# A fused attention and mixture-of-experts kernel: the first q and k transfers issued by two engines

## The chip, the cores and the metric

The kernel runs on one core of a Trainium2 chip. A core has TensorE (PE, matrix products and transposes), VectorE (DVE), ScalarE (ACT), GpSimd (POOL), SyncE (SP, which issues transfers) and 16 DMA engines that all of the core's transfers share. The metric is the device time of one execution in microseconds (us); lower is better. Times of the profile count from the first instruction of the profiled execution.

## The reference

Sliding-window attention with a few "sink" keys, then two mixture-of-experts layers over its output:

```python
scores = scale * np.matmul(q, k.transpose(0, 1, 3, 2))          # (2, 8, 768, 64) q, k, v
keep = (pos[None, :] < n_sink) | ((rel >= 0) & (rel < window))  # n_sink = 4, window = 128
scores = np.where(keep, scores, -1e9)
a = softmax(scores)                                             # rows, 1e-9 added to the sum
x = a @ v                                                       # -> (1536, 512)
x = sum over 4 experts of p[:, e] * (relu(x @ w1[e]) @ w2[e])
x = for each token, its best of 8 experts: gate * (relu(x @ w1b[e]) @ w2b[e])
```

`n_sink` and `window` are inputs, two 64-bit integers in HBM: the kernel reads them on the chip, builds its masks from them, and chooses between a narrow path (taken here) and a general one.

## The kernel before

The program runs in three stages: attention over eight pairs of heads (to about 120 us), the first expert layer (about 120 to 680 us), the second one with its routing (to the end). The change lies in the first ten microseconds, in `Attention.__init__`, before the planned loop over the pairs of heads.

For the first pair (`g = 0`) q and k come in two halves of the sequence: `h0` is the first three blocks of 128 positions, `h1` the last three. `load(g, n, z)` issues two transfers, one for each head of the pair (`x` = 0, 1); `n` is 0 for q and 1 for k. A transfer of one half and one head is 128 x 3 x 64 floats, 98,304 bytes. `ksr` holds the first eight keys of all 16 heads (8 x 16 x 64 floats, 32,768 bytes); `words` gets `n_sink` and `window`, each broadcast to 128 partitions as 8 bytes.

All of these are issued on SP, in the order in which they are written. Each transfer signals its landing on one of eight semaphores (DMAHW0 to DMAHW7) that are used in turn. A transfer that takes a semaphore for the second time is not issued before the first transfer on it has landed: the issuing engine stands and waits.

PE starts with 26 products of a zero tile (`busy`, tile `dum`), whose result nobody reads. Then, written out by hand:

- PE transposes the first half of q (L324), runs 6 idle products, transposes the first half of k (L338) and the first pair's eight sink keys (L340, it needs `ksr`), and runs 18 idle products;
- ScalarE loads its function table for the exponential (L242, with a one-element activation `warm`), then rounds the transposed q (`q_hi`, L328) and the transposed k with its sink keys (`k_hi`, L343);
- VectorE forms the remainder of q (`q_lo`, L332), then turns `words` into floats (L140 to L143), computes the flag `fi` that chooses the path (L269 to L272), forms the remainder of k (`k_lo`, L347) and makes the masks (L291 to L294);
- every engine loads `fi` into a register (`values_load`, L276). On PE this load stands behind the 18 idle products and ahead of the transposes of the second half of q, so PE's further work waits for `fi`.

From there on an event planner (`Order`) has set the order; it is the same before and after.

Of the kernel before, what the change touches and what calls it, by code (L numbers as in the profile page):

```python
# [29 lines left out]
NS = 8  # L30
# [38 lines left out]
class Constants:  # L69


    def __init__(s, nc, cp, ident, emb, tau, probs, en):
        s.nc, s.cp, s.ident, s.en = nc, cp, ident, en
        s.p = cp.tile([P, NT, E1], F32, name="pr")
        s.ta = cp.tile([E2, 1], F32, name="ta")
        nc.sync.dma_start(out=s.p, in_=probs.rearrange("(t p) e -> p t e", p=P))
        s.emb = emb
        nc.sync.dma_start(out=s.ta, in_=tau.partition_broadcast(E2))

        def iota(name, shape, pattern, base, cm):  # L80
            t = cp.tile(shape, F32, name=name)
            nc.gpsimd.iota(t, pattern=pattern, base=base, channel_multiplier=cm, **IOTA)
            return t

        s.w8 = iota("w8", [P, 4, E2], [[0, 4], [-1, E2]], E2, 0)
        s.row = iota("row", [P, P], [[1, P]], 0, 0)
        s.col = iota("colc", [P, E2 * NT], [[1, E2 * NT]], -E2 * NT, 0)
        s.tok = iota("tok", [P, NT], [[P, NT]], 1, 1)
        s.slot = cp.tile([1, NT - 1], F32, name="slotn")
        nc.gpsimd.iota(s.slot, pattern=[[P, NT - 1]], base=P, channel_multiplier=0, **IOTA)  # L90
        s.one = cp.tile([P, 1], F32, name="one")
        nc.gpsimd.tensor_scalar(s.one, s.tok[:, 0:1], 1.0, None, ALU.is_equal)
        s.tr = iota("tr", [P, P], [[1, P]], 0, -1)
        s.tri = cp.tile([P, P], BF16, name="tri")
        s.on = cp.tile([P, P], BF16, name="on")
        s.enT = cp.tile([P, 4, E2], F32, name="enT")
        nc.gpsimd.tensor_scalar(s.tri, s.tr, 0.0, None, ALU.is_gt)
        nc.gpsimd.memset(s.on, 1.0)
# [37 lines left out]
def int64_as_float(nc, tp, i, n):  # L136

    V = nc.vector
    f = tp.tile([P, n, 2], F32, name="i64f")
    V.tensor_copy(f, i)  # L140
    t = tp.tile([P, n], F32, name="i64t")
    V.scalar_tensor_tensor(t, f[:, :, 0], 0.0, f[:, :, 1], ALU.is_lt, ALU.add)
    V.scalar_tensor_tensor(t, t, 4294967296.0, f[:, :, 0], ALU.mult, ALU.add)  # L143
    return t
# [62 lines left out]
class Attention:  # L207


    def __init__(s, tc, st, c0, ps, q, k, v, n_sink, window, x, ident):  # L210

        s.tc, s.nc = tc, tc.nc
        s.q, s.k, s.v, s.x, s.ident = q, k, v, x, ident
        nc = s.nc
        c1 = st.enter_context(tc.tile_pool(name="a1", bufs=1))
        s.qk = [[c1.tile([P, 6, 2, HD], F32, name=f"{n}r{i}") for i in range(2)] for n in "qk"]
        s.vt = [c1.tile([P, 6, 2, HD], F32, name=f"vt{n}") for n in range(3)]
        s.qs = [c1.tile([P, 2, S], F32R, name=f"qs{n}") for n in range(2)]
        s.kk = [c1.tile([P, 2, 2, KW // 2], F32R, name=f"kk{n}") for n in range(2)]
        s.ksr = c1.tile([NS, NH, HD], F32, name="ksr")  # L220
        s.vsr = [c1.tile([P, 4, P], F32, name=f"vsr{n}") for n in range(2)]
        s.pp = ps.tile([P, 2, 512], F32, name="prep")
        s.xo = [ps.tile([P, 512], F32, name=f"xo{a}") for a in range(2)]
        V, A, G = nc.vector, nc.scalar, nc.gpsimd
        s.dum = c1.tile([P, P], BF16, name="dum")
        V.memset(s.dum, 0.0)
        s.busy(s.xo[1], 26)
        words = c0.tile([P, 2, 2], I32, name="words")
        h0, h1 = slice(0, 3), slice(3, 6)
        s.load(0, 0, h0)  # L230
        s.load(0, 1, h0)
        for i, src in enumerate((n_sink, window)):
            nc.sync.dma_start(out=words[:, i], in_=src.bitcast(I32).partition_broadcast(P))
        nc.sync.dma_start(out=s.ksr, in_=k[:, :, 0:NS, :].rearrange("b h s d -> s (b h) d"))
        s.load(0, 0, h1)
        s.load(0, 1, h1)
        s.load(1, 0)
        s.load(1, 1)
        s.vload(0)
        e = c1.tile([1, 1], F32, name="warm")  # L240
        V.memset(e, 0.0)
        A.activation(e, e, AF.Exp)  # L242
        s.rel = c1.tile([P, 2 * P], F32, name="rel")
        s.key = c1.tile([P, P], F32, name="key")
        G.iota(s.rel, pattern=[[-1, 2 * P]], base=P, channel_multiplier=1, **IOTA)
        G.iota(s.key, pattern=[[1, P]], base=0, channel_multiplier=0, **IOTA)
        G.affine_select(
            out=s.rel, in_=s.rel, pattern=[[-1, 2 * P]], compare_op=ALU.is_ge, fill=3.0e38, base=P, channel_multiplier=1
        )
        s.sk = [c1.tile([P, 4, 32], F32, name=f"sk{n}") for n in range(2)]  # L250
        s.masks = c1.tile([P, 4, W], F32, name="masks")
        for t in s.sk:
            G.memset(t, 0.0)
        for t in s.vsr:
            G.memset(t, 0.0)
        G.memset(s.masks[:, 0, P:], -1.0e30)
        G.memset(s.masks[:, 1, 2 * P :], -1.0e30)
        s.q_pe(0, s.pp[:, 0], 0)
        s.busy(s.xo[1], 6)
        s.k_pe(0, s.xo[0], 0)  # L260
        s.busy(s.xo[1], 18)
        s.q_hi(0, s.pp[:, 0], 0)
        s.k_hi(0, s.xo[0], 0)
        s.q_lo(0, s.pp[:, 0], 0)
        nw = int64_as_float(nc, c0, words, 2)
        s.nsf, s.wf = nsf, wf = nw[:, 0:1], nw[:, 1:2]
        fl = c1.tile([1, 2], F32, name="fl")
        fi = c1.tile([1, 1], I32, name="fi")
        V.tensor_scalar(fl[:, 0:1], nsf[0:1], float(NS), None, ALU.is_le)  # L269
        V.tensor_scalar(fl[:, 1:2], wf[0:1], -1.0, 128.0, ALU.mult, ALU.add)  # L270
        V.scalar_tensor_tensor(fl[:, 1:2], wf[0:1], -1.0, fl[:, 1:2], ALU.add, ALU.mult)
        V.scalar_tensor_tensor(fi, fl[:, 1:2], 0.0, fl[:, 0:1], ALU.is_ge, ALU.mult)  # L272
        s.k_lo(0, s.xo[0], 0)
        s.make_masks(c1)
        s.vsload(0)
        s.narrow = nc.values_load(fi[0:1, 0:1], min_val=0, max_val=1)  # L276
# [22 lines left out]
        A.copy(masks[:, 3, P : P + NS], snk[:, :NS])  # L299
        A.copy(masks[:, 3, P + NS :], win[:, P:])  # L300

    def load(s, g, n, z=slice(0, 6)):
        b, h0 = divmod(g * 2, H)
        for x in range(2):
            s.nc.sync.dma_start(
                out=s.qk[n][g % 2][:, z, x, :], in_=(s.q, s.k)[n][b, h0 + x].rearrange("(c p) d -> p c d", p=P)[:, z]
            )

# [840 lines left out]
class Moe2:  # L1149
# [113 lines left out]
    def second(s, w, x, fl, more):  # L1263
# [16 lines left out]
        s.slot(x, w, hooks)  # L1280

    def begin(s, psT, w, x, own, load):

        V, A, G, R = s.nc.vector, s.nc.scalar, s.nc.gpsimd, s.R
# [259 lines left out]
```

## Time and profile before

| | |
|---|---|
| median of 3 runs | 895.85 us (894.11 to 896.01) |
| profiled execution | 898.2 us, of which its span from first to last instruction 896.4 us |
| PE | busy 869.3 us, 97% of the span |
| VectorE, ScalarE, GpSimd | 417.4, 302.1 and 193.1 us |
| mean granted clock of PE | 0.987 of full speed |

In the timeline a row is a start, a duration, an engine, the line of the kernel, the operation, what it writes and reads, and in brackets how long the engine was idle before it and what ended that. "SPq" rows are transfers being issued, not the transfers themselves. In the table of windows each row is a stretch of time: its length, then the busy time of each engine, then the granted clock of PE (1.00 is 2.4 GHz, 0.50 is 1.2 GHz), the busy share of the DMA engines and GB/s.

### The profile page before, as it was taken

Reading aid. Unit: us, or ns where it says so; the run is one execution under the profiler, and the core shown is the slowest. Engines: PE = TensorE matmul, PEld = TensorE weight load, DVE = VectorE, ACT = ScalarE, POOL = GpSimd, SP = SyncE. Lnnn points to the kernel's source line nnn. Section 1 sums busy time; section 2 is a strip of 40 time slices with the busy share of each in tenths; the row PEclk is TensorE's granted clock in tenths of the full one; section 3 lists DMA queues with packets and bytes.
Section 4 is the critical chain, followed back from the end, with each engine's and each line's share of the span. In section 5 each row is a group of like instructions: output and inputs, shape, how many; then the busy total and the mean of one; then the engine's idle time right before and its main releaser. Section 6 shows DMA issues by size and latency. Waiting matters only on the chain. (4 is left out here: it accounts for less than half of the span.)

```text
span 896.4 us, 11797 instructions
## 1 busy us (share of the span) xinstructions
PE 869.3 (97%) x4266; PEld 681.0 (76%) x4266; DVE 417.4 (47%) x1003; ACT 302.1 (34%) x662; POOL 193.1 (22%) x291
## 2 busy tenths in 40 slices
PE   8999999999999999999999999999999799999995
PEld 6676777878888888888888888888887577777774
DVE  5787753121233121233121234858646768937510
ACT  5787852010302010302010303111233557636421
POOL 4576510000000000000000000030223846726310
PEclk8999999999999999999999999999999999999998
DMA  7567110030022000023000022101345577946200
GB/s 135 107 137 154 46 46 2 1 119 1 0 94 94 1 0 1 1 94 94 1 1 1 0 71 84 58 0 48 118 136 170 163 254 222 307 141 205 70 32 24
DMA packets 84400, 72.47 MB, mean 81 GB/s; under 512 B 43860, under 2 KB 68436, under 8 KB 84328
## 3 DMA queue, kind: packets, MB, share of 16 engines
q1 hardware_dynamic: 81448, 65.25, 25.0%
q0 software_dynamic: 2880, 6.30, 2.1%
q8 instruction: 40, 0.66, 0.3%
q14 instruction: 32, 0.26, 0.1%
HBM read 67.58 MB, written 7.09 MB: 83 GB/s over the span
## 5 line engine op out<-in xcount | busy, mean ns | idle before, releaser
L998 PE MATMUL ph<-x,wA 128*128 128x512 f32 x1152 | 273.0, 397 | 1.5 <-DVE h L1004 1.5
L1082 PE MATMUL po<-wA,h 128*128 128x512 f32 x1152 | 273.3, 396 | 0.0
L998 PEld LDWEIGHTS ph<-x,wA 128*128 128x128 f32 x1152 | 216.5, 188 | 54.2 <-DVE h L1004 1.9
L1082 PEld LDWEIGHTS po<-wA,h 128*128 128x128 f32 x1152 | 215.1, 188 | 51.7
L1003 ACT ACTIVATE h<-ph 128x512 fp32r<-128x512 f32 x96 | 57.4, 598 | 389.4 <-PE ph L998 384.1
L1004 DVE SCALAR_TENSOR_TENSOR h<-ph,h 128x512 fp32r<-128x512 f32 x96 | 66.4, 692 | 175.9 <-ACT h L1003 175.9
L60 POOL TENSOR_TENSOR gn<-gn,rss 128x4 f32<-128x4 f32 x9 | 1.8, 198 | 444.1 <-DVE gn L58 443.6
L682 DVE TENSOR_TENSOR wA<-raw,wA 128x512 fp32r<-128x512 f32 x107 | 77.3, 750 | 2.5 <-ACT wA L676 1.7
L1092 DVE SCALAR_TENSOR_TENSOR acc<-po,pr,acc 128x512 f32<-128x512 f32 x36 | 27.0, 750 | 109.9 <-PE po L1082 109.9
L676 ACT CAST wA<-raw 128x512 fp32r<-128x512 f32 x115 | 65.5, 618 | 4.0 <-DMA raw<-in_moe_w_dram 3.6
L408 POOL TENSOR_TENSOR P<-P,r 128x264 f32<-128x264 f32 (+1 forms) x87 | 54.2, 647 | 43.9 <-DVE r L403 24.5
L1219 PE MATMUL po<-wA,ht 128*128 128x512 f32 x216 | 58.3, 409 | 0.6 <-DVE ht L1213 0.6
L1213 DVE TENSOR_TENSOR ht<-hT,ht 128x512 fp32r<-128x512 f32 x30 | 20.7, 691 | 67.9 <-ACT ht L1212 67.8
L389 ACT ACTIVATE P<-m,nm 128x264 f32<-128x264 f32 x96 | 49.0, 512 | 8.3 <-DVE nm L383 7.8
L1219 PEld LDWEIGHTS po<-wA,ht 128*128 128x128 f32 x216 | 39.7, 192 | 9.4 <-DVE ht L1213 1.5
L383 DVE CUSTOM_DVE_ANT_0 m<-sc,masks 128x264 f32<-128x264 f32 x96 | 38.5, 429 | 14.0 <-PE sc L370 12.3
L1196 PE MATMUL ph<-wA,xt 128*128 128x512 f32 x168 | 42.7, 401 | 2.0 <-PEq L1346 1.0
L682 DVE TENSOR_TENSOR wB<-raw,wB 128x512 fp32r<-128x512 f32 x44 | 40.3, 940 | 4.4 <-ACT wB L676 3.3
L771 DVE CUSTOM_DVE_ANT_0 rj<-acc,raw 128x512 f32<-128x512 f32 x64 | 40.1, 687 | 0.2
L370 PE MATMUL sc<-kk,qs 64*128 64x264 f32 x288 | 38.2, 329 | 0.7 <-DVE nm L383 0.7
L1219 PE MATMUL po<-wB,ht 128*128 128x512 f32 x144 | 38.6, 405 | 0.3 <-DVE ht L1213 0.3
L1196 PEld LDWEIGHTS ph<-wA,xt 128*128 128x128 f32 x168 | 30.6, 188 | 10.7 <-DVE xt L1122 1.9
(220 smaller groups left out, 852.1 us busy)
## 6 DMA issues: line engine op xcount, KB each, us to landing
raw<-in_moe_w_dram SPq DMA_DIRECT2D x96, 512.0 KB
vt<-in_v_dram SPq DMA_DIRECT2D x16, 192.0 KB
xs<-acc SPq DMA_DIRECT2D x12, 256.0 KB
qr<-in_q_dram SPq DMA_DIRECT2D x14, 192.0 KB
kr<-in_k_dram SPq DMA_DIRECT2D x14, 192.0 KB
raw<-en SPq DMA_DIRECT2D x4, 512.0 KB
vsr<-in_v_dram SPq DMA_DIRECT2D x64, 2.0 KB
qr<-in_q_dram SPq DMA_DIRECT2D x4, 96.0 KB
```

The costliest lines, as they stand in the source:

```text
L383: V.tensor_tensor_reduce(m, t["sc", par][:, :W], masks[:, VAR[i]], -1.0, 3.0e38, ALU.add, ALU.min, t["nm"][:, par, i : i + 1])
L389: A.activation(t["P"][:, par, i], t["m", par, i], AF.Exp, scale=-1.0, bias=t["nm"][:, par, i : i + 1], accum_out=t["su"][:, par, i : i + 1],)
L408: eng.tensor_tensor(y, y, t["r", a][:, par].unsqueeze(2).to_broadcast([P, b - a, W]), ALU.mult)
L676: eng.copy(dst()[:, 0], r)
L682: eng.tensor_tensor(d[:, 1], r, d[:, 0], ALU.subtract)
L771: s.nc.vector.tensor_tensor_reduce(j, s.acc[:, tt], s.eb[e], 1.0, 0.0, ALU.mult, ALU.add, s.dl[:, tt, e : e + 1])
L998: s.nc.tensor.matmul(ph, s.wA.w1(a, k, f * P)[:, :P], s.x[:, b, k, tb * TB : (tb + 1) * TB], start=(n == 0), stop=(n == 11))
L1003: s.nc.scalar.activation(t[:, 0], ph, AF.Relu)
L1004: s.nc.vector.scalar_tensor_tensor(t[:, 1], ph, 0.0, t[:, 0], ALU.max, ALU.subtract)
L1082: nc.tensor.matmul(po, hs[f][:, a, t * P : (t + 1) * P], wA.w2(b, f), start=(n == 0), stop=(n == 23))
L1196: nc.tensor.matmul(ph[b], x[:, a, kk], w.w1(c, kk, b * 512), start=(kk == 0 and n == 0), stop=(kk == 3 and n == 2),)
L1219: nc.tensor.matmul(s.po[0], ht[b][:, a, c * P : (c + 1) * P], w.w2(d, f), start=(f == 0 and n == 0), stop=(f == 7 and n == 2),)
```

## The change

ScalarE issues the transfers of the second head of the first pair (`x = 1`), for both halves of q and k; SP keeps those of the first head. `ksr` moves to ScalarE, behind the first halves and ahead of the second halves. The two scalar inputs, which were issued between the halves, now come behind the second halves, still on SP. Nothing is added or taken away: there are as many transfers as before, with the same bytes.

```diff
         h0, h1 = slice(0, 3), slice(3, 6)
-        s.load(0, 0, h0)
-        s.load(0, 1, h0)
+        two = (nc.sync, nc.scalar)
+        s.load(0, 0, h0, two)
+        s.load(0, 1, h0, two)
+        nc.scalar.dma_start(out=s.ksr, in_=k[:, :, 0:NS, :].rearrange("b h s d -> s (b h) d"))
+        s.load(0, 0, h1, two)
+        s.load(0, 1, h1, two)
         for i, src in enumerate((n_sink, window)):
             nc.sync.dma_start(out=words[:, i], in_=src.bitcast(I32).partition_broadcast(P))
-        nc.sync.dma_start(out=s.ksr, in_=k[:, :, 0:NS, :].rearrange("b h s d -> s (b h) d"))
-        s.load(0, 0, h1)
-        s.load(0, 1, h1)
         s.load(1, 0)
         s.load(1, 1)
-    def load(s, g, n, z=slice(0, 6)):
+    def load(s, g, n, z=slice(0, 6), queues=None):
         b, h0 = divmod(g * 2, H)
         for x in range(2):
-            s.nc.sync.dma_start(
+            (queues or [s.nc.sync] * 2)[x].dma_start(
```

ScalarE at the start of the program, before (in these listings a row is a line of the kernel, an operation, what it writes and reads and its shape; the semaphores that it waits for stand in brackets; `qr` and `kr` are q and k as they come in):

```order
L242 ACT_TABLE_LOAD
L242 ACTIVATE warm<-warm 1x1 [waits DVE_49]
L328 ACTIVATE qs_97<-prep 128x384 [waits PE_49]
L343 CAST kk_99<-xo_105 128x392 [waits PE_49]
L295 COPY masks<-win 128x128 [waits DVE_49]
```

and after:

```order
L306 DMA qr_90<-in_q_dram 128x3x64
L306 DMA kr_92<-in_k_dram 128x3x64
L233 DMA ksr<-in_k_dram 8x16x64
L306 DMA qr_90<-in_q_dram 128x3x64 [waits DMAHW2_49]
L306 DMA kr_92<-in_k_dram 128x3x64 [waits DMAHW4_49]
L243 ACT_TABLE_LOAD
L243 ACTIVATE warm<-warm 1x1 [waits DVE_49]
L329 ACTIVATE qs_97<-prep 128x384 [waits PE_49]
L344 CAST kk_99<-xo_105 128x392 [waits PE_49]
```

Five transfers now stand ahead of the table load and of `q_hi`, and the last two of them wait for earlier transfers to land.

SP at the start of the program, before:

```order
L305 DMA qr_90<-in_q_dram 128x3x64 x2
L305 DMA kr_92<-in_k_dram 128x3x64 x2
L233 DMA words<-in_n_sink_dram 128x2
L233 DMA words<-in_window_dram 128x2
L234 DMA ksr<-in_k_dram 8x16x64
L305 DMA qr_90<-in_q_dram 128x3x64
L305 DMA qr_90<-in_q_dram 128x3x64 [waits DMAHW0_49]
```

and after:

```order
L306 DMA qr_90<-in_q_dram 128x3x64
L306 DMA kr_92<-in_k_dram 128x3x64
L306 DMA qr_90<-in_q_dram 128x3x64
L306 DMA kr_92<-in_k_dram 128x3x64
L237 DMA words<-in_n_sink_dram 128x2
L237 DMA words<-in_window_dram 128x2 [waits DMAHW0_49]
L306 DMA qr_91<-in_q_dram 128x6x64 [waits DMAHW1_49]
```

The two scalar inputs still stand behind four transfers of 98,304 bytes on SP; the second one has got a wait for the first transfer of q.

PE after, at the transposes of the first half of k, where the semaphores of k and of `ksr` can be read:

```order
L339 MATMUL xo_105<-ident,kr_92 128x128 [waits DMAHW3_49,DMAHW2_49]
L339 MATMUL xo_105<-ident,kr_92 128x128 x2
L341 MATMUL xo_105<-ident,ksr 128x8 [waits DMAHW4_49]
L285 LDWEIGHTS dum
L285 MATMUL xo_106<-dum 128x128
```

PE's own order has not moved; DMAHW2 and DMAHW3 belong to the first half of k, DMAHW4 to `ksr`.

## Rows read from the trace of the kernel before

**Rows 1.** The page, sections 1 and 2: PE's share, granted clock in 40 slices.

```profile
PE 869.3 (97%) x4266; PEld 681.0 (76%) x4266; DVE 417.4 (47%) x1003; ACT 302.1 (34%) x662; POOL 193.1 (22%) x291
PEclk8999999999999999999999999999999999999998
```

**Rows 2.** Table of windows over the attention stage; its first line names the columns.

```profile
core 0: us, PE busy (x) PEld busy (x) DVE busy (x) ACT busy (x) POOL busy (x), PEclk, DMA share, GB/s
0.00:10.00 10.00, 6.78 (x60) 6.06 (x60) 2.90 (x14) 2.82 (x6) 3.69 (x19) 0.94 0.62 119
10.00:20.00 10.00, 9.07 (x54) 6.51 (x52) 7.69 (x34) 7.54 (x25) 5.48 (x13) 0.84 0.80 128
...
30.00:60.00 30.00, 30.00 (x251) 20.91 (x250) 23.63 (x95) 24.20 (x72) 19.18 (x35) 1.00 0.47 106
```

**Rows 3.** Timeline of the first microseconds: transfers as SP issues them.

```profile
0.83 0.97 SPq L305 DMA_DIRECT2D qr<-in_q_dram  x2
...
1.84 1.02 SPq L305 DMA_DIRECT2D kr<-in_k_dram  x2
...
2.90 0.49 SPq L233 DMA_DIRECT2D words<-in_n_sink_dram  x1
...
3.43 0.43 SPq L233 DMA_DIRECT2D words<-in_window_dram  x1
...
3.91 0.38 SPq L234 DMA_DIRECT2D ksr<-in_k_dram  x1
```

**Rows 4.** The same timeline: PE's products and transposes.

```profile
1.07 2.96 PE L284 MATMUL xo<-dum 128*128 128x128 bf16 x26 [1.07 <-DVE warm L241]
...
4.17 0.87 PE L324 MATMUL prep<-ident,qr 128*128 128x128 f32 x3
...
5.45 0.50 PE L338 MATMUL xo<-ident,kr 128*128 128x128 f32 x3
...
7.95 0.22 PE L340 MATMUL xo<-ident,ksr 8*128 8x8 f32 x1 [2.01 <-DMA ksr<-in_k_dram]
...
8.11 1.48 PE L284 MATMUL xo<-dum 128*128 128x128 bf16 x18
...
9.38 0.85 PE L324 MATMUL prep<-ident,qr 128*128 128x128 f32 x3
```

**Rows 5.** The same timeline: ScalarE and VectorE.

```profile
0.81 1.28 ACT L242 ACT_TABLE_LOAD   x1 [0.81 <-PEq L1539]
...
2.10 0.20 ACT L242 ACTIVATE warm<-warm 1x1 f32<-1x1 f32 x1
...
5.08 0.49 ACT L328 ACTIVATE qs<-prep 128x384 fp32r<-128x384 f32 x1 [2.77 <-PE prep L324]
...
5.60 0.56 DVE L332 SCALAR_TENSOR_TENSOR qs<-prep,qs 128x384 fp32r<-128x384 f32 x1 [4.58 <-ACT qs L328]
...
7.45 0.17 DVE L140 CAST i64f<-words 128x4 f32<-128x4 int32 x1 [1.29 <-DMA words<-in_window_dram]
...
8.46 0.15 DVE L272 SCALAR_TENSOR_TENSOR fi<-fl 1x1 int32<-1x1 f32 x1
```

**Rows 6.** Instructions on tile fi, durations ns min/median/max, then starts: PE's register load.

```profile
L276 PEldq TENSOR_LOAD <-fi x1: 497/497/497, 8.7 to 8.7; - x1
```

**Rows 7.** Table of windows, columns as in rows 2: what the transfers moved.

```profile
1.90:2.90 1.00, 1.00 (x12) 1.00 (x11) 0.00 (x0) 0.39 (x2) 1.00 (x4) 1.00 0.68 155
2.90:3.90 1.00, 1.00 (x11) 0.86 (x9) 0.00 (x0) 0.00 (x0) 0.78 (x4) 1.00 0.80 181
...
4.40:6.40 2.00, 1.55 (x12) 1.25 (x11) 0.56 (x1) 0.49 (x1) 0.00 (x0) 1.00 0.05 1
...
9.40:11.40 2.00, 2.00 (x13) 1.43 (x12) 1.00 (x5) 1.58 (x7) 1.91 (x9) 0.50 1.39 219
```

**Rows 8.** Timeline: six score products at the low and at the full clock.

```profile
10.16 1.03 PE L370 MATMUL sc<-kk,qs 64*128 64x264 f32 x6
...
14.80 0.64 PE L370 MATMUL sc<-kk,qs 64*128 64x264 f32 x6
```

## The prediction

> **What bounds the kernel now.** I read the page first: PE is busy for 97% of the span and its clock is full except near the start and the end [rows 1]. The table of windows then says where a change of the first transfers can still matter: from 30 to 60 us PE is busy for 30.00 of 30.00 us, while in the first ten it lacks 3.2 us and in the next ten 0.9 [rows 2]. So PE is the bound of the whole attention stage, its order is fixed, and a microsecond won or lost before PE's first real work is carried on to the end, nearly one to one. The question is only when PE gets going.
>
> The timeline of the first ten microseconds answers that, and the reader is to look for the wait that ends last, not for the longest one. The longest is plain: PE has transposed the first half of k at 5.95 and stands still for 2.01 us until `ksr` lands at 7.95 [rows 4]. But behind it stand 18 idle products, to 9.59, and behind those the load of `fi`, which PE performs from 8.7 to 9.2; only then come the transposes of the second half of q, at 9.38 [rows 4, 6]. `fi` is written at 8.46 to 8.61 by VectorE, at the end of a chain that began at 7.45, when `words` had landed [rows 5]. Thus two transfers gate PE here: `ksr` at 7.95, and `words` at 7.45, whose chain of 1.16 us and register load end at about the same time as the idle products behind `ksr`. Take away one, and the other still holds PE until about 9.3.
>
> **What the change does to `ksr`.** It is issued as ScalarE's third transfer, at about 1.8 instead of 3.91 (two issues of about 0.5 us ahead of it, by SP's pace of 0.97 for two [rows 3]). It no longer stands behind `words`. That matters: from 4.40 to 6.40 the DMA engines moved 1 GB/s at a share of 0.05, though more transfers had been issued, so the two small broadcasts passed alone and held up what stood behind them on SP [rows 3, 7]. From issue to use the first q pair took 4.14 - 1.3 = 2.8 us for its second transfer, `ksr` itself 7.95 - 3.91 = 4.0 us [rows 3, 4]. Landing of `ksr` after: between 1.8 + 2.8 = 4.6 and 1.8 + 4.0 = 5.8. I take 4.9, near the lower end, because no broadcast stands ahead of it. Either end is before 5.95, where PE wants it: the wait of 2.01 us is gone, the 18 idle products run from about 6.15 to 7.6, and `k_hi` is done early. The gain on PE's path is nothing, since PE then stands at the load of `fi`.
>
> **What it does to q and k.** Two issuers at 0.5 us each bring the pairs out in half the time. It hides behind the 26 idle products, which run to 4.03 while the transposes of q start at 4.17 [rows 4]: at most 0.1 us, and not on the path.
>
> **What it does to `words`.** They are issued at the same place on SP, behind four transfers of 98,304 bytes, so at 2.90 and 3.43 as before. The second now waits for the first q transfer to land; by 0.83 + 2.8 = 3.6 that adds 0 to 0.2 us. What is new is the company: before, 393,216 bytes were ahead of them and had passed by 4.4, at 155 and 181 GB/s, the pace of one issuer [rows 7]. After, ScalarE's first two transfers and `ksr` pass at the same time, 622,592 bytes in all. At the 219 GB/s that the engines gave when they had enough to do [rows 7] this takes 2.8 us from 1.9, to 4.7. So `words` move later by 0.3, with bounds of 0 (the other queue doesn't disturb them) and 0.9 (ScalarE's second halves get between them too: 196,608 bytes more at 219 GB/s).
>
> Here a page bears on the case. The Trainium skill, "DMA: Bandwidth & Descriptors", section "Issuing engines are not separate DMA queues", says that transfers of all issuers run on the same 16 DMA engines and interleave, and that a second issuer saves only issue time. By that rule `words` go to the 0.3 and 0.9 ends; without it they stay at 0.
>
> **What it does to ScalarE.** This is the added wait. Five transfers stand ahead of the table load, and behind it `q_hi`. The fourth waits for a first-half transfer of k, the fifth for `ksr`. Behind them queue the table load, `warm`, `q_hi` and `k_hi` on ScalarE; behind `q_hi` VectorE's `q_lo`, and in VectorE's order the cast of `words` comes after `q_lo`. The chain, from rows: k lands at about 1.3 + 2.8 = 4.1, the fourth issue takes until 4.6; `ksr` at 4.9, the fifth issue until about 5.45; table load 1.28, to 6.73; `warm` 0.20, to 6.95; `q_hi` 0.49, to 7.45; `q_lo` 0.56, to 8.0 [rows 5]. Before, `q_lo` ended at 6.16, long before `words`. The cast therefore starts at 8.0 instead of 7.45: +0.55. With `ksr` at 4.6 it is +0.25, with 5.8 it is +1.45. The table load alone used to cost nothing, because ScalarE had nothing else to do from 0.81 to 5.08; that cover is gone.
>
> A second page would make this longer. The Trainium skill, "ScalarE: Activation LUTs", section "What ACT_TABLE_LOAD costs", gives 1283 ns for the load, as here, and a drain of about 1380 ns besides. In this trace the next activation began at 2.10, right behind the load [rows 5], so no drain shows; by the page the cast would start 1.38 us later still.
>
> **The sum.** The cast starts at the later of `words` (7.45 + 0.3) and `q_lo` (+0.55): +0.55. From there VectorE's chain to `fi`, PE's register load and the second half of q follow as before. `k_lo` gains 0.1 (its input is ready before `fi`), but the first scores wait for PE's transposes, so that gives nothing. PE's idle gap moves from 5.95..7.95 to about 7.6..9.8 and stays about as long. The granted clock fell to 1.2 GHz after the old gap: windows of 9.4 to 11.4 show 0.50 [rows 7], and six score products took 1.03 us there against 0.64 at the full clock [rows 8]. With a gap as long, I take the same fall, a little later, and no change from it. Everything later on SP (second pair, v) is issued earlier and is not waited for. The profiled execution: 898.2 + 0.55 = 898.75. The median of the runs shown is 2.35 below the profiled execution; with the same step it becomes 895.85 + 0.55 = 896.4.
>
> **The rivals.** What a measurement of this kernel can tell from no change is about 0.2%, 1.8 us, so the bounds are 894.05 and 897.65.
>
> - *ScalarE becomes the gate for good* (slower). Its place is the fifth transfer, which waits for `ksr`. If `ksr` lands late, the table load, `q_hi`, `q_lo`, the cast and `fi` all move with it, one to one. It decides from the point where the cast starts at 7.45 + 1.8 = 9.25, that is with `ksr` at about 6.2. If `ksr` lands as late as before, at 7.9, the chain reads 8.45, 9.73, 9.95, 10.45, 11.0: +3.55, 899.4. For it: the engines are shared, and the only landing of `ksr` in this trace took 4.0 us. Against it: these 4.0 us contain the 2.0 us of the broadcasts, which stand behind it now. At 4.0 us from its new issue it still lands at 5.8. Chance 0.15.
> - *The table load drains* (slower): q_lo ends at 8.0 + 1.38 = 9.4 and the sum is +1.95, 897.8, just beyond the bound. The row on `warm` speaks against it. Chance 0.03.
> - *The clock doesn't fall* (faster). PE is busy from 1.07 to 7.6 without the 2.01 us gap, and the later gap could end before the clock falls. Then three groups at the start of the second ten (transposes of q and of k, six scores) each gain about 0.35 to 0.4, 1.1 us, and the low stretch that follows at 20 us, of which PE's busy 10.00 of 10.00 us make a path, may give as much again or more: -2.2 + 0.55, about 894.2, and a little further with luck. For it: the mean clock is 0.94 and 0.84 in the first two tens [rows 2]. Against it: PE now waits for `fi` for as long as it waited for `ksr`. Chance 0.09.
> - *Nothing moves at all*: `words` land at 7.45, `ksr` early enough that `q_lo` is done by then. 895.85, within the forecast's bounds.
>
> **How the numbers follow.** Within 0.2%: the forecast and the last rival, 0.73. Slower by over 0.2%: 0.15 + 0.03 = 0.18. Faster by over 0.2%: 0.09. The forecast's own range is 895.85 to 897.3 (+0 to +1.45), widened by the 1.9 us over which the three runs already spread. For 8 in 10 I reach to 894.2 on the clock's side and to 898.8 on ScalarE's, about `ksr` at 7.3.
>
> **What the profile after would show.** Right: no wait of PE for `ksr`; ScalarE's table load at 5 to 6 instead of 0.81; `q_lo` directly followed by the cast at 7.7 to 8.5; PE standing after its 18 idle products until `fi`; the second transposes of q at about 9.9. Wrong: the cast before 7.3, or PE's second transposes of q before 9.2 (then `words` gained from something that I have not seen); table load beyond 6.5 (the slower rival); a clock of 1.00 throughout the first 20 us (the faster one).

## The result, and the profile after

The changed kernel takes 902.17 us (median of 7 runs, 899.63 to 903.46); the kernel before took 896.25 us beside it (7 runs). The ratio is 1.0056, with a 95% interval of 1.0039 to 1.0072: slower by 5 us by the ratio (the medians lie 5.9 apart), outside the range of the prediction.

On the page almost nothing has moved. PE is as busy as before [rows 1]; only its granted clock in the first two slices is lower. The first line is section 1, the second the clock in 40 slices:

```profile
PE 869.6 (97%) x4266; PEld 681.2 (76%) x4266; DVE 412.1 (46%) x1003; ACT 302.3 (34%) x662; POOL 193.6 (22%) x291
...
PEclk7899999999999999999999999999999999999998
```

The loss is over early. A milestone says so: the first and the last start of the products that compute the hidden layer of the experts, in the view of one line (instructions, durations in ns, first and last start). The first row is of before, the second of after:

```profile
L998 PE MATMUL ph<-x,wA x1152: 391/397/499, 124.2 to 644.3; 128*128 128x512 f32 x192
```

```profile
L999 PE MATMUL ph<-x,wA x1152: 391/397/500, 127.5 to 647.6; 128*128 128x512 f32 x192
```

They begin 3.3 us later and then take the same 520.1 us. So what these two executions lost by then, they lost in the attention stage. The pair shows only a part of the slowdown: before's 898.2 us lies above all 7 runs beside it (highest 898.13), and after's 899.63 is the quickest of its 7. Of the 3.3 us even these two keep only 1.3 at the end of their spans (896.4 and 897.7); the rest comes back in the last stage, where the clock from 680 to 720 us is 0.91 before and 0.96 after.

The timeline of after, SP's and ScalarE's transfers (start, duration, engine, line; compare [rows 3]):

```profile
0.81 0.48 ACTq L306 DMA_DIRECT2D qr<-in_q_dram  x1
...
1.90 0.64 ACTq L233 DMA_DIRECT2D ksr<-in_k_dram  x1
...
2.90 0.49 SPq L237 DMA_DIRECT2D words<-in_n_sink_dram  x1
...
3.79 0.34 SPq L237 DMA_DIRECT2D words<-in_window_dram  x1
...
4.17 1.02 SPq L306 DMA_DIRECT2D qr<-in_q_dram  x2
...
4.91 0.39 ACTq L306 DMA_DIRECT2D qr<-in_q_dram  x1
...
5.46 0.40 ACTq L306 DMA_DIRECT2D kr<-in_k_dram  x1
```

The same timeline, PE (compare [rows 4]; PEld is its weight load), and PE's register load of `fi` (compare [rows 6]):

```profile
5.48 0.13 PEld L341 LDWEIGHTS xo<-ident,ksr 8*128 8x128 f32 x1 [0.24 <-DMA ksr<-in_k_dram]
5.48 0.22 PE L341 MATMUL xo<-ident,ksr 8*128 8x8 f32 x1
...
5.64 1.18 PE L285 MATMUL xo<-dum 128*128 128x128 bf16 x18
...
10.56 0.31 PEld L325 LDWEIGHTS prep<-ident,qr 128*128 128x128 f32 x3 [3.92 <-DVE snk L293]
10.60 0.52 PE L325 MATMUL prep<-ident,qr 128*128 128x128 f32 x3 [3.78 <-DMA kr<-in_k_dram]
```

```profile
L277 PEldq TENSOR_LOAD <-fi x1: 501/501/501, 9.5 to 9.5; - x1
```

The wait of 2.01 us for `ksr` is gone, as the change intends. In its place PE stands still for 3.78 us after its 18 idle products, and the second transposes of q start at 10.60 instead of 9.38. The register load, from 9.5 to 10.0, doesn't account for all of it; the row names a transfer besides.

The same timeline, ScalarE and VectorE (compare [rows 5]):

```profile
5.89 1.28 ACT L243 ACT_TABLE_LOAD   x1 [5.89 <-DMA ksr<-in_k_dram]
...
7.19 0.20 ACT L243 ACTIVATE warm<-warm 1x1 f32<-1x1 f32 x1
7.30 0.46 ACT L329 ACTIVATE qs<-prep 128x384 fp32r<-128x384 f32 x1
...
7.79 0.56 DVE L333 SCALAR_TENSOR_TENSOR qs<-prep,qs 128x384 fp32r<-128x384 f32 x1 [6.78 <-ACT qs L329]
8.27 0.16 DVE L140 CAST i64f<-words 128x4 f32<-128x4 int32 x1
...
9.27 0.15 DVE L273 SCALAR_TENSOR_TENSOR fi<-fl 1x1 int32<-1x1 f32 x1
```

The cast of `words` is now directly behind `q_lo`, with no wait for a transfer: ScalarE's chain sets it.

Then the table of windows (columns as in [rows 2]): first over the attention stage's beginning, then around the transfers (compare [rows 7]).

```profile
0.00:10.00 10.00, 5.74 (x57) 5.14 (x57) 2.15 (x12) 2.22 (x4) 2.98 (x15) 1.00 0.67 129
10.00:20.00 10.00, 8.73 (x42) 6.57 (x43) 6.37 (x28) 6.75 (x24) 4.32 (x13) 0.57 0.76 125
20.00:30.00 10.00, 9.95 (x50) 7.16 (x49) 5.79 (x26) 6.19 (x19) 3.59 (x6) 0.58 0.88 168
30.00:40.00 10.00, 10.00 (x78) 6.81 (x77) 7.66 (x31) 8.21 (x24) 7.45 (x14) 1.00 0.16 26
```

```profile
3.90:4.90 1.00, 1.00 (x11) 0.92 (x9) 0.00 (x0) 0.00 (x0) 0.00 (x0) 1.00 1.09 172
4.90:7.30 2.40, 1.92 (x25) 1.46 (x22) 0.00 (x0) 1.40 (x3) 0.00 (x0) 1.00 0.09 9
7.30:9.30 2.00, 0.00 (x0) 0.00 (x0) 1.33 (x8) 0.82 (x3) 0.00 (x0) 1.00 1.23 252
```

After the gap the clock is 0.57 and 0.58 over 20 us, where before it was 0.84 [rows 2] and 0.71:

```profile
20.00:30.00 10.00, 10.00 (x61) 7.03 (x61) 6.45 (x33) 7.87 (x27) 5.04 (x11) 0.71 0.89 171
```

This row of before holds 61 PE instructions of the attention in 10.00 us of work, that of after 50 in 9.95. PE is busy in both; it gets less done.

To compare kernels I use two quantities. **Half-clock time**: a window of 10 us with a mean clock c holds 20 · (1 - c) us at the lower of the two levels, 1.2 GHz, if it is at the full 2.4 GHz otherwise. Over the first 40 us that is 1.2 + 3.2 + 5.8 = 10.2 us before and 8.6 + 8.4 = 17.0 us after. **Start**: the start of PE's second transposes of q, 9.38 before and 10.60 after.

### The profile page after: what moved, and what is told of

It reads as the page before. It is cut to its first block, busy times and chain, and to the rows that moved or that the text cites. A ratio compares the mean times of both kernels' runs of the same rounds, so it can differ in the third digit from the quotient of the medians.

```text
span 897.7 us, 11797 instructions
## 1 busy us (share of the span) xinstructions
PE 869.6 (97%) x4266; PEld 681.2 (76%) x4266; DVE 412.1 (46%) x1003; ACT 302.3 (34%) x662; POOL 193.6 (22%) x291
## 5 line engine op out<-in xcount | busy, mean ns | idle before, releaser
L683 DVE TENSOR_TENSOR wB<-raw,wB 128x512 fp32r<-128x512 f32 x44 | 38.1, 890 | 4.4 <-ACT wB L677 3.3
L1197 PEld LDWEIGHTS ph<-wA,xt 128*128 128x128 f32 x168 | 30.6, 188 | 10.7 <-DVE xt L1123 1.9
```

Source lines behind the costliest of these rows:

```text
L683: eng.tensor_tensor(d[:, 1], r, d[:, 0], ALU.subtract)
L1197: nc.tensor.matmul(ph[b], x[:, a, kk], w.w1(c, kk, b * 512), start=(kk == 0 and n == 0), stop=(kk == 3 and n == 2),)
```

## The experiments

Five theories stand in the expectations. Theory 1: most of the loss is PE's clock, which falls after the longer gap. Theory 2: it is only the later start. Theory 3: the late table load of ScalarE is what holds the cast. In the second set, A and B ask what makes the start late. Theory A: the two broadcasts of `words` hold up what is queued behind or beside them, so their place makes the loss. Theory B: the two queues don't hold each other up, and the cast comes late behind ScalarE's table load. Idle products (`s.busy`) compute nothing that is used, so kernels with more or fewer of them compute the same. The columns: ratio to the kernel before with its interval; start S, half-clock time L in the first 40 us and milestone M of the profiled execution; and H, the half-clock time of a whole execution, which is 2 · (1 - clock) · span, averaged over the runs of the kernel. H takes in the low clock of the later stages too: in the profiled executions it is 6 to 15 us longer than L.

| kernel | ratio [95%] | median us | S | L | M | H |
|---|---|---|---|---|---|---|
| before | 1 | 897.1, 898.2, 898.4 | 9.38 | 10.2 | 124.2 | 19.6, 23.5, 22.7 |
| after | 1.0056 [1.0039, 1.0072] | 902.17 | 10.60 | 17.0 | 127.5 | 32.7 |
| e1 | 0.9976 [0.9951, 1.0001] | 895.01 | 10.11 | 6.8 | 123.8 | 14.8 |
| e2 | 0.9984 [0.9959, 1.0009] | 895.54 | 8.94 | 0 | 120.5 | 19.9 |
| e3 | 1.0041 [1.0022, 1.0060] | 899.90 | 10.32 | 17.0 | 127.4 | 30.6 |
| e4 | 1.0058 [1.0035, 1.0082] | 903.24 | 11.73 | 20.4 | 129.5 | 33.4 |
| e5 | 1.0025 [1.0001, 1.0049] | 899.22 | 10.03 | 17.0 | 126.9 | 29.3 |
| e6 | 0.9985 [0.9959, 1.0011] | 896.38 | 9.25 | 17.2 | 126.2 | 21.9 |
| e7 | 0.9975 [0.9948, 1.0001] | 895.62 | 9.50 | 0 | 121.1 | 19.7 |
| e8 | 1.0007 [0.9988, 1.0025] | 898.35 | 9.23 | 24.0 | 128.4 | 30.6 |
| e9 | 1.0031 [1.0013, 1.0049] | 901.09 | 10.46 | 17.0 | 127.3 | 31.1 |
| e10 | 0.9984 [0.9960, 1.0008] | 898.48 | 10.69 | 0 | 122.0 | 22.6 |
| e11 | 0.9952 [0.9929, 0.9975] | 894.28 | 8.25 | 6.8 | 121.9 | 17.4 |
| e12 | 0.9943 [0.9927, 0.9959] | 893.55 | 8.37 | 0 | 119.6 | 15.8 |

The three values of before belong to e1 to e4, e5 to e8 and e9 to e12, which ran beside it; for the runs of before beside after no clock is on record.

### e1: after, with the gap filled by idle products

```diff
-        s.busy(s.xo[1], 18)
+        s.busy(s.xo[1], 66)
```

> The changed kernel with 66 instead of 18 idle products between PE's transposes of the first k and its load of the path flag: 48 more, about 3.2 us at the 66 ns that one took, so that PE does not stand still from 6.8 to 10.0 us. Nothing that PE waits for comes earlier. Theory 1 (most of the 5.9 us is PE's clock: the gap grew from 2.0 to 3.8 us and the clock then stayed at 1.2 GHz from 11.4 to 28.5 us): the low stretch is gone or shrinks to under 7 us, and the time falls to 893 to 897, a ratio to the kernel before of 0.997 to 1.001. Theory 2 (the time goes into the later start itself and into later waits, the clock is a companion): no gain, 901 to 903, ratio 1.005 to 1.008.

Measured: 0.9976, against 1.0056 without the 48 products; the intervals are apart. The timeline of PE and the clock from 10 to 20 us:

```profile
5.60 3.86 PE L285 MATMUL xo<-dum 128*128 128x128 bf16 x66
...
10.11 0.52 PE L325 MATMUL prep<-ident,qr 128*128 128x128 f32 x3 [0.65 <-DVE win L292]
```

```profile
10.00:20.00 10.00, 8.85 (x57) 6.52 (x59) 8.45 (x36) 8.09 (x27) 6.43 (x17) 0.93 0.68 118
```

PE starts its second transposes only 0.49 us earlier than in after, still 0.73 later than before, and the whole loss is gone. By theory 2 the kernel would have stayed slower than before. So theory 1 holds for this kernel: most of what the gap costs, it costs through the clock that follows it.

### e2: before, with its gap filled

```diff
+        if g == 0 and a == 0:
+            s.busy(s.xo[1], 30)
```

These stand ahead of the transpose of `ksr`.

> The kernel before with 30 idle products put into PE's 2.0 us wait for the sinks' keys. Theory 1: the clock does not fall at 8.8 us, and perhaps not at 19 us either; of 10.2 us at half clock up to 10 go, so 2 to 5 us are gained, ratio 0.995 to 0.998. Theory 2: PE's wait for the sinks' keys is unchanged, the time too, ratio 0.999 to 1.001.

Measured: 0.9984 [0.9959, 1.0009]. In the profiled execution the clock is 1.00 in all of the first 40 us and the milestone comes 3.7 us earlier, at 120.5; but H over its runs is 19.9, as in before's own (19.6). So filling the old gap of 2.01 us gains nothing that these runs can tell. Theory 1 expected a gain (0.995 to 0.998) from a clock that stays up; four of the 12 runs still have a mean clock of 0.981 to 0.984, and where it fell in them is not on record. The wait is thus not all that decides about the clock.

### e3: the second halves all on SP

```diff
-        s.load(0, 0, h1, two)
-        s.load(0, 1, h1, two)
+        s.load(0, 0, h1)
+        s.load(0, 1, h1)
```

> The changed kernel, but ScalarE issues only its two first halves and the sinks' keys; both second halves of both heads go out on SP ahead of the two scalar inputs. No transfer on ScalarE waits for a semaphore, so its table load starts at about 2.5 instead of 5.9 us. If the later table load is what holds the cast of the scalar inputs (theory 3), the cast comes at the landing of the scalar inputs. They are now issued behind six transfers on SP, about 1 us later, so they land at about 8.5 to 9, the flag at about 10, and PE's gap stays at 3 to 4 us: 900 to 903, ratio 1.003 to 1.008. The second halves, no longer behind the scalar inputs, land before 7 us and PE does not wait for them. If theory 3 were the main cost, the ratio would be under 1.002.

Measured: 1.0041. With only three transfers ahead of it, ScalarE's table load is early again, and still the cast is about as late as in after (8.27):

```profile
2.58 1.28 ACT L243 ACT_TABLE_LOAD   x1 [2.58 <-issue]
...
8.41 0.17 DVE L140 CAST i64f<-words 128x4 f32<-128x4 int32 x1 [2.62 <-DMA words<-in_window_dram]
...
10.32 0.88 PE L325 MATMUL prep<-ident,qr 128*128 128x128 f32 x3 [2.84 <-DMA kr<-in_k_dram]
```

Now VectorE waits 2.62 us for `words`, which SP issues at 4.07 and 4.75, behind six transfers. Theory 3 falls as the sole cause: two chains, ScalarE's and the words', end at 8.3 to 8.4, and taking one away leaves the other.

### e4: the new order, one issuer

```diff
-        two = (nc.sync, nc.scalar)
+        two = (nc.sync, nc.sync)
...
-        nc.scalar.dma_start(out=s.ksr, in_=k[:, :, 0:NS, :].rearrange("b h s d -> s (b h) d"))
+        nc.sync.dma_start(out=s.ksr, in_=k[:, :, 0:NS, :].rearrange("b h s d -> s (b h) d"))
```

> All transfers on SP, as before the change, but in the changed order: first halves, sinks' keys, second halves, scalar inputs. This does the move of the scalar inputs without the second issuer. The scalar inputs are issued behind nine transfers, at about 5.2 and 5.7 instead of 2.9 and 3.4 us, and land at about 9.7 (before: 7.4). The sinks' keys land at about 5.3. PE's gap runs from about 6.8 to 11.7, so its clock falls for long: theory 1 expects 901 to 906, ratio 1.005 to 1.011, and slower than the changed kernel by the 1 to 2 us that the second issuer saves. Theory 2 expects the delay alone, 2.3 us, ratio 1.002 to 1.004.

Measured: 1.0058, as much as the whole change. `words` are issued at 5.41 and 5.94, and the cast waits for them:

```profile
9.82 0.17 DVE L140 CAST i64f<-words 128x4 f32<-128x4 int32 x1 [4.14 <-DMA words<-in_window_dram]
```

Of all kernels its start is the latest (11.73) and its half-clock time H the longest (33.4). Moving the words to the end is bad by itself; the second issuer brings the start back from 11.73 to 10.60, but the ratio is the same.

### e5: two issuers, the words back between the halves

```diff
         s.load(0, 1, h0, two)
+        for i, src in enumerate((n_sink, window)):
+            nc.sync.dma_start(out=words[:, i], in_=src.bitcast(I32).partition_broadcast(P))
...
-        for i, src in enumerate((n_sink, window)):
-            nc.sync.dma_start(out=words[:, i], in_=src.bitcast(I32).partition_broadcast(P))
```

> The changed kernel with the two scalar inputs issued between the halves again, as before the change (SP: two first halves, two scalar inputs, two second halves). ScalarE keeps its five transfers. If the place of the scalar inputs makes the loss (theory A), they are issued at 1.8 and 2.4 us, pass from about 3 to 5.3 and land at about 6.3; ScalarE's sinks' keys and second halves are held up meanwhile, so the keys land at about 6 to 7 and the table load starts only then: the cast comes at about 9 behind the remainder of q. Then PE's gap is no shorter than after the change, 3 to 4 us, and the time 900 to 904, ratio 1.003 to 1.008. If the two queues do not hold each other up (theory B), the keys land at 5.4 as after the change, the cast comes at 8.3 behind the table load, the flag at 9.4, and the gap is 3.2: about 900. Either way it should not be faster than before; under 1.000 would say that the late place of the scalar inputs alone is the loss.

Measured: 1.0025 [1.0001, 1.0049]. `words` are issued at 1.83 and 2.36, over a microsecond earlier than in after, and the cast moves by 0.14 us only, to 8.13: it stands behind `q_lo`, and that behind a table load at 5.76. The gap is 3.47 us. So the words' place alone is not the loss: with them early the cast stands behind ScalarE's five transfers and the table load, near the 8.3 that B expected. The ratio is lower than after's 1.0056, but the intervals overlap.

### e6: after, the words issued by GpSimd

```diff
-            nc.sync.dma_start(out=words[:, i], in_=src.bitcast(I32).partition_broadcast(P))
+            nc.gpsimd.dma_start(out=words[:, i], in_=src.bitcast(I32).partition_broadcast(P))
```

> The changed kernel with the two scalar inputs issued on GpSimd, at about 1.3 us, instead of last on SP. Theory A (the broadcasts hold up what SP and ScalarE have queued behind or beside them, and gate PE by the flag): the second halves land at about 7 instead of 10.5, the scalar inputs at about 4 to 5, the cast comes behind the remainder of q at about 7 to 8, the flag at 8 to 9, PE's gap shrinks from 3.8 to 1.5 to 2.5 us, 893 to 898, ratio 0.997 to 1.002. If broadcasts issued on GpSimd pass as slowly and hold up the rest in the same way, the q pairs land late and the ratio stays above 1.004.

Measured: 0.9985, as before within its interval. The broadcasts are issued at 1.58 and 2.31. ScalarE's fourth transfer is now issued at 3.28 instead of 4.91, so the table load comes 0.9 us earlier than in after, and the cast with it, still behind `q_lo`:

```profile
4.97 1.28 ACT L243 ACT_TABLE_LOAD   x1 [4.97 <-DMA kr<-in_k_dram]
...
7.34 0.16 DVE L140 CAST i64f<-words 128x4 f32<-128x4 int32 x1
```

This is theory 3 in the place where it does decide: with the words early, the gate is ScalarE's chain (e11 takes this chain away as well). The profiled execution had much half-clock time (17.2 in 40 us), the runs on the mean did not (H 21.9); a single profile is a poor witness for the clock.

### e7: before, the words issued by GpSimd

The same edit in the kernel before.

> The kernel before (one issuer, SP), only the two scalar inputs issued on GpSimd. Theory A: the sinks' keys are issued at 2.9 instead of 3.9 and no longer stand behind the broadcasts, so they land at about 5.3 instead of 7.9; the flag is ready by 7 since ScalarE's table load is early; PE's wait for the keys (2.0 us) and the wait for the flag both go, PE's second transposes of q start at 7.5 instead of 9.4 and the clock need not fall at 9 us: 890 to 895, ratio 0.992 to 0.998. If the broadcasts hold up SP's transfers from GpSimd too, nothing is gained: 0.999 to 1.003.

Measured: 0.9975 [0.9948, 1.0001]. The cast comes at 6.45 instead of 7.45, but k now lands late (PE waits 0.96 us for it and transposes it at 6.60 instead of 5.45) and the start is 9.50, not 7.5 as expected: the 18 idle products behind k and `ksr` run from 7.61 to 9.7, though `fi` is being written at 7.46. A microsecond won on one chain was lost on the other; no gain that can be told from nothing.

### e8: before, without the 18 idle products behind the gap

```diff
-        s.busy(s.xo[1], 18)
```

> The kernel before without the 18 idle products that stand behind the sinks' keys. Nothing that PE waits for moves: its second transposes of q still start at about 9.3 us, behind the load of the flag. It only stands still longer, 3.2 instead of 2.0 us. Theory 1 (the loss is the clock after a longer gap): slower than before by 2 to 6 us, ratio 1.002 to 1.007, with a mean clock near 0.982 as after the change. Theory 2 (the later start): no change, 0.999 to 1.001.

Measured: 1.0007 [0.9988, 1.0025]. The profile looked like a clear yes for theory 1, with 24 us at half clock and a milestone of 128.4, 4.2 later than before, though the start is even 0.15 earlier:

```profile
20.00:30.00 10.00, 10.00 (x48) 7.16 (x47) 5.09 (x22) 5.82 (x17) 4.14 (x7) 0.50 0.83 158
```

The time doesn't follow. By the ratio it is 0.6 us slower, inside what theory 2 expected (0.999 to 1.001) and below what theory 1 did (1.002 to 1.007). H rose from 23.5 to 30.6 us; by the prices worked out below that is worth 1.7 us (runs of one kernel) to 2.6 us (medians), and the upper end of the interval is 2.2 us. So the clock was lost and its price not seen: this run doesn't bear theory 1 out, and it speaks for the lower price.

### e9: after, unaltered, once more

> The changed kernel itself, unaltered, beside the next three on the same chip and with every run's clock. Both theories expect the first result again: ratio 1.004 to 1.007. Theory 1 expects a mean clock of about 0.981 beside 0.985 to 0.989 of the kernel before.

Measured: 1.0031 [1.0013, 1.0049], below the first measurement and the 1.004 that was expected at least, but with an interval that overlaps the first. Start 10.46, half-clock time 17.0 and H 31.1 came out as before. The slowdown is between 0.13% and 0.72% by the two intervals together.

### e10: after, with half of the filling

```diff
-        s.busy(s.xo[1], 18)
+        s.busy(s.xo[1], 42)
```

> The changed kernel with 42 instead of 18 idle products: half of the first experiment's filling, so that PE stands still for about 2.1 instead of 3.8 us before its second transposes of q. The start is as late as after the change. Theory 1: the time falls between the changed kernel and the first experiment, ratio 0.999 to 1.003, and the mean clock lies between 0.981 and 0.9925. Theory 2: as the changed kernel, 1.004 to 1.007.

Measured: 0.9984 [0.9960, 1.0008] with a gap of 1.67 us, a little under the 0.999 to 1.003 of theory 1 and far from theory 2. The profiled execution is at full clock:

```profile
6.09 2.93 PE L285 MATMUL xo<-dum 128*128 128x128 bf16 x42
...
10.69 0.52 PE L325 MATMUL prep<-ident,qr 128*128 128x128 f32 x3 [1.67 <-DVE masks L294]
```

```profile
10.00:20.00 10.00, 8.35 (x57) 6.17 (x59) 7.87 (x36) 8.00 (x27) 5.84 (x16) 1.00 0.80 132
```

The 12 runs of this one kernel fall in two groups by their mean clock: four at 0.994 to 0.996, with 892.92 to 895.08 us, and eight at 0.981 to 0.986, with 897.47 to 900.10 us. No run lies between. Same instructions, same order: with the clock, some 5 us part them, as much as the change under study costs. By the means of the groups (H of 9.4 and 29.2, 893.6 and 898.9 us) a microsecond at half clock goes with 0.27 us. The profiled one is of the quick group.

### e11 and e12: words on GpSimd, second halves on SP; and 30 more idle products

```diff
-        s.load(0, 0, h1, two)
-        s.load(0, 1, h1, two)
+        s.load(0, 0, h1)
+        s.load(0, 1, h1)
...
-            nc.sync.dma_start(out=words[:, i], in_=src.bitcast(I32).partition_broadcast(P))
+            nc.gpsimd.dma_start(out=words[:, i], in_=src.bitcast(I32).partition_broadcast(P))
```

e12 has besides:

```diff
-        s.busy(s.xo[1], 18)
+        s.busy(s.xo[1], 48)
```

> The changed kernel with the two scalar inputs on GpSimd and the second halves of both heads on SP: ScalarE issues only two first halves and the sinks' keys, and its table load starts at 2.5 us. With the scalar inputs on GpSimd alone the cast came at 7.3, directly behind the remainder of q; now that remainder is done by 5.7 and the scalar inputs land at 6.4 to 6.7, so the cast comes at 6.5 to 6.8, the flag at 7.7 to 8.0, PE's second transposes of q at 8.4 to 8.7, if the second halves have landed by then (8.5 with the scalar inputs on GpSimd alone). PE's gap is 1.5 us. Theory 1: 891 to 896, ratio 0.994 to 0.998. If ScalarE's late table load cost nothing, the ratio stays at that of the run with the scalar inputs on GpSimd alone, 0.9985.

> The same with 48 instead of 18 idle products, which closes PE's gap of 1.5 us (30 more at about 62 ns are 1.9 us, so that PE's second transposes of q start at 8.7 to 9.0, 0.3 later). Theory 1: the clock stays up at least to 15 us in nearly all executions, 890 to 894, ratio 0.992 to 0.996, the best of all. Theory 2: 0.3 us slower than without them.

Measured: 0.9952 [0.9929, 0.9975] and 0.9943 [0.9927, 0.9959]: both beat the kernel before. In e11 both late chains are early at once, and the cast is 1.1 us ahead of before:

```profile
6.33 0.17 DVE L140 CAST i64f<-words 128x4 f32<-128x4 int32 x1 [0.56 <-DMA words<-in_window_dram]
...
8.25 0.52 PE L325 MATMUL prep<-ident,qr 128*128 128x128 f32 x3 [0.85 <-DVE win L292]
```

In e12 the rest of the gap is filled too; PE has no wait from the idle products to q, and the clock is full in the first 40 us:

```profile
5.68 2.85 PE L285 MATMUL xo<-dum 128*128 128x128 bf16 x48
...
8.37 0.52 PE L325 MATMUL prep<-ident,qr 128*128 128x128 f32 x3
```

```profile
10.00:20.00 10.00, 8.88 (x62) 6.68 (x62) 8.80 (x41) 8.72 (x27) 5.38 (x11) 1.00 0.56 97
```

e12 is the best version seen, 893.55 us. From e11 to e12 the intervals overlap, so what the 30 products add there is not shown.

### All profiles in one sum

The 14 milestones of the table follow, by least squares, M = 119.9 + 0.96 · (S - 8.37) + 0.32 · L. A microsecond of later start is carried on one to one, and a microsecond at half clock costs a third of one (PE is not the only engine with work in that stage). For after against before: 0.96 · 1.22 + 0.32 · 6.8 = 1.2 + 2.2 = 3.4 us, measured 3.3. The medians give nearly the same prices without the milestones: ratio times 898 us is fitted by 1.06 (with a standard error of 0.4) a microsecond of S and 0.36 of H, with residues up to 1.9 us, the largest in e8. For after, with about 22 us for H of before, that is 1.06 · 1.22 + 0.36 · 10.7 = 1.3 + 3.9 = 5.2 us, and the ratio of 1.0056 is 5.0 us. For after's second measurement, e9, the same prices give 1.06 · 1.08 + 0.36 · 8.4 = 4.2 us, and the ratio of 1.0031 is 2.8.

A third price leaves the differences between kernels out. Among the 226 runs with a clock on record, each taken against the mean of its own kernel and set, a microsecond of H goes with 0.24 us (standard error 0.015). By it the 10.7 us of after are 2.6 of its 5.0 us. So about half (runs of one kernel), two thirds (milestones) or three quarters (medians) of the slowdown go through the clock; the exact share stays open.

PE's longest wait between its first transposes and S goes together with H across the kernels. After, e3, e4, e5 and e9, with waits of 2.84 to 4.68 us, have an H of 29.3 to 33.4, and so has e8, where waits of 1.86 and 1.22 us follow each other closely (30.6). Before, e6 and e10, with waits of 1.67 to 2.31 us, have 19.6 to 23.5; e1, e2, e7, e11 and e12, with less than 1 us, 14.8 to 19.9.

## Why the prediction was wrong, step by step

- **What bounds the kernel**: right. What happens before PE's first real work is carried on one to one (slopes 0.96 and 1.06).
- **`ksr`**: right. The forecast had it landed at 4.9, with bounds of 4.6 and 5.8; PE took it at 5.48, after its weight load had waited 0.24 us. The wait of 2.01 us is gone and gave nothing on PE's path, as forecast.
- **The first halves of q and k**: right; PE transposes q at 3.86 instead of 4.17, and it is not on the path.
- **`words`**: the second issue came at 3.79, later by 0.36 instead of 0 to 0.2. In after their landing can't be read, since the cast stands behind `q_lo`. Where the cast does wait for them, it comes 4.0 us after the second issue (before, 3.43 to 7.45), 3.7 (e3) and 3.9 (e4). By that they landed at 7.5 to 7.8 in after, an estimate, around the forecast's 7.75. (Its upper bound of 0.9 is a slip: the 0.9 of ScalarE's second halves comes on top of the 0.3. It wasn't reached.)
- **ScalarE's chain**: right in kind, too small. The forecast for the cast was +0.55; it was +0.82 (8.27), and +0.98 in e9 (8.43). The fourth transfer, which waits for a first half of k issued at 1.3, was issued at 4.91, not at 4.1, so the table load came at 5.89, not 5.45. The 2.8 us that the sum took from issue to landing come from a start of PE that stood behind idle products, and were 3.6 here. What stands behind the load, to the cast, took 2.38 us, a little less than the 2.55 of the sum. `warm` began at 7.19, 0.02 us after the load's end: the drain of about 1380 ns that the Trainium skill, "ScalarE: Activation LUTs", section "What ACT_TABLE_LOAD costs", adds to it shows neither at 0.81 nor at 5.89, and the rival that went by it doesn't stand.
- **A wait that the sum lacks.** The sum took the second half of q for hidden ("the second half of q follow as before"). But its second head is ScalarE's fourth transfer, issued at 4.91, when SP had already begun to issue the second pair of heads (from 4.17). The queues of after by what they moved (packets, MB, share of 16 engines; q1 is SP's, q10 ScalarE's), first from 4.9 to 7.3, then from 7.3 to 9.3:

```profile
q1 hardware_dynamic: 317, 0.02, 9.1%
```

```profile
q1 hardware_dynamic: 1594, 0.39, 90.6%
q10 hardware_dynamic: 464, 0.12, 32.2%
```

  ScalarE's queue first moves nothing, then shares the engines with SP's. PE's register load ended at 10.0, and the transposes still waited until 10.56. From the start of `fi` to S it takes 0.92 us in before and 0.89 in e1, but 1.33 in after, 1.02 in e9 and 1.48 in e10. Up to 8.3 us ScalarE's queue had moved next to nothing in just these three, and much in e1. From 4.9 to 8.3, after first, then e1:

```profile
q10 hardware_dynamic: 12, 0.00, 0.4%
```

```profile
q10 hardware_dynamic: 543, 0.13, 18.6%
```

  In e9 and e10 it had moved no packet, in e5 and e6, where `fi` to S takes 0.90 and 0.91, it had moved 680 and 672. What the transposes waited for is named `qr` only in e9 (after names `kr`, e10 VectorE):

```profile
10.46 0.88 PE L325 MATMUL prep<-ident,qr 128*128 128x128 f32 x3 [3.07 <-DMA qr<-in_q_dram]
```

  So the start is +1.22 instead of +0.55: 0.8 from the cast, 0.4 from a landing, by these rows that of q's second head; no run isolates it. Here the rule of the Trainium skill, "DMA: Bandwidth & Descriptors", section "Issuing engines are not separate DMA queues", agrees with the windows: the two queues shared one set of engines. The prediction weighed it for `words` alone, where it mattered least.
- **The step that failed** is the sentence on the gap: it "moves from 5.95..7.95 to about 7.6..9.8 and stays about as long", and "With a gap as long, I take the same fall, a little later, and no change from it." The gap was 3.78 us, from 6.82 to 10.60. Each end was off by 0.8 us. At the front the idle products began at 5.64, not 6.15, since k and `ksr` were done earlier, and took 1.18 us, not 1.45, at the full clock. At the back stand the cast and q's landing. Removing one wait made PE's work ahead of the gap end earlier while the gate behind it moved later; both add to the gap. And the fall was not the same: 17.0 us at half clock in the first 40 against 10.2, H of 31 to 33 against about 22. e1 shows the price by taking it away: a gate nearly as late (10.11), the gap filled, and the loss is gone. How much of the 5 us is the clock's stays open between half and three quarters.
- **The rivals.** "ScalarE becomes the gate for good" forecast 899.4 by a late `ksr`, with the cast beyond 9.25; the cast was at 8.27 and `ksr` early, so it was slower for another reason. "The clock doesn't fall" had the right quantity and the wrong sign: it saw that the clock at the start is worth 2 us and more, and let the change only win there. The mirror image, a longer gap and a longer fall, was not among the cases, and the range of 894.2 to 898.8 had no term for it.

## What to carry over

When a wait is taken away ahead of a second gate, work out the engine's new idle stretch from both ends: what stands ahead of it ends earlier, what stands behind may come later, and a longer idle stretch of TensorE can cost more through the clock after it than through itself. A tiny transfer that gates a chain should get its own early issue, not the end of a queue, and an engine that computes should not have transfers that wait ahead of its first work. Where one execution's clock differs from the next, judge the clock by the mean over the runs, not by one profile.

## What the runs showed of the hardware

- **Half clock costs a quarter to a third.** A microsecond at 1.2 GHz costs 0.32 us in the attention stage (milestones); over the whole kernel it goes with 0.24 us (runs of one kernel) or 0.36 us (medians of the kernels).
- **The same program, two clocks.** e10's 12 runs are at a mean clock of 0.994 to 0.996 or at 0.981 to 0.986, some 5 us apart, with nothing between.
- **The tiny broadcasts take 4 us.** The cast comes 3.7 to 4.0 us after the second of two transfers of 1 KB has been issued, on SP or (e11: issued at 2.30, cast at 6.33) on GpSimd. While they pass on SP's queue the engines move 1 GB/s (before, 4.40 to 6.40) to 9 GB/s (after, 4.90 to 7.30). That they hold up the other issuer's transfers was seen to coincide (ScalarE's queue empty from 4.90 to 7.30); no run isolates it.
- **The table load has no drain here**: the next activation begins 0.01 to 0.02 us after it, early or late.
